# A fused attention, Fourier mixing and expert kernel on one core: raw weights loaded ahead, a second fold, split stores, factors on VectorE

## The chip, the cores and the metric

The kernel runs on one core of a Trainium2 chip. The metric is the device time of one execution in microseconds (us), the median of several runs. Engines are named as in the profile: PE (TensorE matmul), PEld (its weight loads), DVE (VectorE), ACT (ScalarE), POOL (GpSimd), SP (SyncE, which here issues most DMA transfers).

## The reference, cut to what matters

Three stages follow one another; B, H, S, D are 4, 8, 576, 64, so 2304 tokens of 512 features.

```python
# 1 attention, causal window of 128 with a linear bias per head
scores = where(mask, scale * q @ k.T - slope[h] * |i - j|, -1e9)
x = softmax(scores) @ v                      # -> (B, S, 512)
# 2 mixing and a dense MLP (w_ch1 512x2048, w_ch2 2048x512)
u  = x + real(fft(fft(x, axis=1), axis=2))
un = (u - mean(u)) / sqrt(var(u) + 1e-06)
x  = u + relu(un @ w_ch1) @ w_ch2
# 3 one of 8 experts a token (w1 512x1024, w2 1024x512), sticky routing
e  = argmax(x @ w_gate) if s == 0 or sigmoid(x @ w_local) < 0.5 else previous e
out = softmax(x @ w_gate)[e] * (relu(x @ w1[e]) @ w2[e])
```

The dense weights arrive as float64. The kernel reads them as pairs of 32-bit words ("raw words") and makes a high and a low float32 part of each; every dense product is then three matmuls (lines 162, 163, 164: high by high, high by low, low by high).

## The kernel before

**Attention** works on one batch at a time; its q and k come on SP (line 263), v too (line 265). Its rows leave in `xs`, folded about the middle of the sequence: block kt of `xs` holds rows `xa` and the mirrored rows `xb`.

**Mixing** (`mixing`, line 426) computes the real part of the two transforms as cosine and sine products. `fold` (lines 431 to 448) makes on DVE the sum and the difference of `xa` and `xb`, then adds (even part, line 445) and subtracts (odd part, line 446) the upper half of the 512 features onto the lower, mirrored. `zprod` (line 454) is the first product, over the sequence, in blocks of 128 features, with a last column, feature 256, apart in `zn`. The second product, over the features (lines 475 to 479), runs for each of three row blocks kb:

```python
for cs, ps in ((1, pz), (0, pc)):
    for db in range(2):
        nc.tensor.matmul(ps[0:n, 0:K2], lhsT=Z[cs][:, db, c0:c0 + n], rhs=tab2[:, cs, db], ...)
nc.tensor.matmul(pc[0:n, 0:K2], lhsT=zn[:, c0:c0 + n], rhs=alt, start=False, stop=True)
```

K2 is 257. A matmul in float32 shows as two records in the trace. Lines 482 to 489 combine the parts onto `xs` (DVE), and lines 491 to 502 store the rows as `ud`, 128 tokens a tile; one store holds rows 1 to 127 of tile 3 (line 493).

**Normalise** (line 546) loads `u` from `ud` on SP (line 553; not in the first group, whose rows are still in `xs`), takes statistics on DVE (lines 558, 560), makes the factor 1/sqrt(var) and the shift in 12 POOL operations (lines 565 to 573), applies them on ACT (line 577), transposes on PE (line 511) and splits into `xT` (ACT line 158, DVE line 159).

**The MLP** runs on nine groups of 256 tokens. `mlp_first` (line 595) does the first half of the 2048 hidden features with four weight chunks A of 256 and stores a partial sum `pd` (line 612); a later pass does the second half with four chunks B. `convert` (line 224) makes a quarter of a chunk from 512 KB of raw words: a load on SP (line 228) into one of RB = 2 buffers of the tag r64, a scaling on ACT (line 232), three operations on DVE (233 to 235), a cast on ACT (158) and a subtraction on POOL (159). A load waits for its buffer. Chunks live in the pools wpA and wpB, which hold four chunks each.

**Routing and experts.** Routing (lines 784 and following) follows each group of the second half. `early` (line 997) prepares the first 256 tokens of one expert while the last groups run: it loads that expert's weights (`expert_weights`, line 940), its list of slots (`slot_load`, line 981), turns it into row numbers (`slot_ids`, lines 990, 991), gathers the rows on POOL and transposes them on PE. Each `yield` gives way to the other work of the last groups; EL = 7 and EY = 8 count such steps.

**What sets the order.** The opening, mixing of batch 0 and normalise of group 0 (`opening`, line 676), is issued in the written order on PE, DVE, ACT and POOL. Afterwards attention, mixing, conversions and `mlp_first` are lanes of a table of due times, and a scheduler at build time fixes the order on each engine. Every engine then works strictly in that order; SP's queue too.

Of the kernel before, what the change touches and what calls it, by code (L numbers as in the profile page):

```python
# [10 lines left out]
F32 = mybir.dt.float32  # L11
# [12 lines left out]
DM = H * D  # L24
# [28 lines left out]
TB_ = 3  # L53
WB = 3
FL = 2
EY = 8
EL = 7
HB = 4
VL = 3
# [42 lines left out]
def constants():  # L102
    c = {}
    s = np.arange(3 * P).reshape(3, P).T
    k1 = np.arange(K1)
    ok = (s[:, :, None] <= HALF) & (k1[None, None, :] <= HALF)
    ang = (s[:, :, None] * k1[None, None, :]) % S
    tab1 = np.stack([np.where(ok, np.cos(2 * np.pi * ang / S), 0.0),
                     np.where(ok & ((2 * ang) % S != 0), np.sin(2 * np.pi * ang / S), 0.0)], 1)
    d = np.arange(2 * P).reshape(2, P).T  # L110
    k2 = np.arange(K2)
    ok = np.broadcast_to(k2[None, None, :] <= DM // 2, (P, 2, K2))
    ang = (d[:, :, None] * k2[None, None, :]) % DM
    tab2 = np.stack([np.where(ok, np.cos(2 * np.pi * ang / DM), 0.0),
                     np.where(ok & ((2 * ang) % DM != 0), np.sin(2 * np.pi * ang / DM), 0.0)], 1)
    c["tab1"] = tab1.astype(np.float32)
    c["tab2"] = tab2.astype(np.float32)
    c["alt"] = np.where(k2 <= DM // 2, 1.0 - 2.0 * (k2 % 2), 0.0).astype(np.float32)[None]
# [25 lines left out]
    empty = np.zeros((2, NSLOT, 4), np.float32)  # L144
    empty[0, :, 1] = NONE
    c["empty"] = empty
    c["zero"] = np.zeros((4 * P, DM), np.float32)
    return c


def build(ctx, tc, a, out):
# [55 lines left out]
    def weight_tiles(wp):  # L207
        return (wp.tile([P, 2, 4, CB], F32R, tag="w1", name="t1"), wp.tile([P, 2, CB // P, DM], F32R, tag="w2", name="t2"))

    def load_weights64(tiles, w1, w2, c, words):  # L210
        t1, t2 = tiles
        q = CB // 2
        for j in range(2):
            f0 = c * CB + j * q
            s = w1[:, 2 * f0:2 * (f0 + q)].rearrange("(k p) f -> p k f", p=P)
            convert(t1[:, 0, :, j * q:(j + 1) * q], t1[:, 1, :, j * q:(j + 1) * q], s, words)
            yield
        for j in range(CB // P):
            f0 = c * CB + j * P
            s = w2[f0:f0 + P].rearrange("p (k f) -> p k f", k=4)  # L220
            convert(t2[:, 0, j].rearrange("p (k f) -> p k f", k=4), t2[:, 1, j].rearrange("p (k f) -> p k f", k=4), s, words)
            yield

    def convert(hi, lo, src, words):

        k, n = hi.shape[1], hi.shape[2]
        r = wraw.tile([P, k, 2 * n], U32, tag="r64", name="r64", bufs=RB)
        nc.sync.dma_start(out=r, in_=src)
        w = r.rearrange("p k (n t) -> p k n t", t=2)
        wl, y = w[:, :, :, 0], w[:, :, :, 1]  # L230
        t = words().rearrange("p (k n) -> p k n", k=k)
# [13 lines left out]
    ps_s = c1.enter_context(pool("ps_s", 1, space=PSUM))  # L245

    tab1 = cst.tile([P, 2, 3, K1], F32, name="tab1")
    tab2 = cst.tile([P, 2, 2, K2], F32, name="tab2")
    alt = cst.tile([1, K2], F32, name="alt")

    def slab(shape, dt, name, tag, bufs):
        return sl.tile(shape, dt, tag=tag, name=name, bufs=bufs)

    HN = DM // 2
    NB = 5
    SC = -1.0 / math.sqrt(D)

# [168 lines left out]
    def mixing(b):  # L426
# [4 lines left out]
        def fold(kt):  # L431
# [22 lines left out]
        def zprod(part, kt):  # L454
            xf, n = zin[kt]
            for cs, db in part:
                w = P if db < 2 else 1
                if kt == 0:
                    pss[cs, db] = ps_g.tile([P, DM], F32, tag="g", name="zps")
                nc.tensor.matmul(pss[cs, db][0:w, 0:K1], lhsT=xf[0:n, cs, db * P:db * P + w], rhs=tab1[0:n, cs, kt], start=kt == 0, stop=kt == 2)  # L460
# [10 lines left out]
        for kb in range(3):  # L471
# [18 lines left out]
            row = lambda t: ud[GIDX[b, t]]  # L490
            if kb == 0:
                nc.sync.dma_start(out=row(0), in_=xs[0][:, 0])
                nc.sync.dma_start(out=row(3)[1:P], in_=xs[0][1:P, 1])
            elif kb == 1:
                nc.sync.dma_start(out=row(1), in_=xs[1][:, 0])
                nc.sync.dma_start(out=row(2), in_=xs[1][:, 1])
            else:
# [4 lines left out]
                nc.sync.dma_start(out=um[r + 32:r + 64], in_=xs[2][0:32, 1])  # L502
            if kb == 2:
                mixed[0] = b
            yield
# [40 lines left out]
    def normalise(gs, xT, us, src=None):  # L546
# [18 lines left out]
        nc.gpsimd.tensor_scalar_add(v0, mv[:, 0:n, 1], 1.0e-6)
        nc.gpsimd.tensor_tensor(out=v1, in0=v0, in1=half[:, 0:n], op=ALU.pow)
        for _ in range(2):
            nc.gpsimd.tensor_tensor(out=v2, in0=v1, in1=v1, op=ALU.mult)
            nc.gpsimd.tensor_tensor(out=v2, in0=v2, in1=v0, op=ALU.mult)
            nc.gpsimd.tensor_scalar(out=v2, in0=v2, scalar1=-0.5, scalar2=1.5, op0=ALU.mult, op1=ALU.add)  # L570
            nc.gpsimd.tensor_tensor(out=v1, in0=v2, in1=v1, op=ALU.mult)
        nc.gpsimd.tensor_tensor(out=v2, in0=mv[:, 0:n, 0], in1=v1, op=ALU.mult)
        nc.gpsimd.tensor_scalar_mul(v2, v2, -1.0)
        yield
        for i, g in enumerate(gs):
            un = us[i]
# [37 lines left out]
                for _ in pre:  # L614
                    yield ("piece", 0)

    chunksA = [weight_tiles(wpA) for c in range(FA // CB)]
    def tables():

        with tc.issue_after(last["load"].ins):  # L620
# [14 lines left out]

    def conversions():
        for c in range(FA // CB):
            yield from load_weights64(chunksA[c], a["w_ch1"], a["w_ch2"], c, lambda: sm.tile([P, 2 * CB], U32, tag="t64", name="t64", bufs=2))

    END = object()  # L640

# [96 lines left out]
    chunksB = [weight_tiles(wpB) for c in range(FA // CB, FF // CB)]  # L738

    room = lact.tile([P, 4, 2 * CB], U32, tag="xTe", name="t64", bufs=1)  # L740
    turns = iter(range(4 * FF // CB))
    for c in range(FA // CB, FF // CB):
        for _ in load_weights64(chunksB[c - FA // CB], a["w_ch1"], a["w_ch2"], c, lambda: room[:, next(turns) % 4]):
            pass

    wt8 = late.tile([P, E], F32, name="wt8")
# [456 lines left out]
```

## Time and profile before

| | |
|---|---|
| median of 3 runs | 1034.43 us (1032.81 to 1038.68) |
| profiled execution | 1039.1 us, span 1037.4 us, mean granted clock 0.959 |
| opening (0 to 84 us) | PE busy 67.30 us |
| attention and mixing of batches 1 to 3 beside the first MLP half (150 to 330) | PE busy 163.43 of 180 us |
| end of the first half, chunks B made (330 to 450) | PE busy 103.90 of 120 us |
| second half (450 to 700) | PE busy 246.79 of 250 us |
| its end, early expert (700 to 750) | PE busy 43.19 of 50 us |
| experts (750 to 1037) | PE busy 261.94 of 287 us |

The profile follows one execution; times of its instructions are from its own start. [...] Idle time of an engine stands in brackets with what ended it.

### The profile page before, as it was taken

Reading aid. Unit: us, or ns where it says so; the run is one execution under the profiler, and the core shown is the slowest. Engines: PE = TensorE matmul, PEld = TensorE weight load, DVE = VectorE, ACT = ScalarE, POOL = GpSimd, SP = SyncE. Lnnn points to the kernel's source line nnn. Section 1 sums busy time; section 2 is a strip of 40 time slices with the busy share of each in tenths; the row PEclk is TensorE's granted clock in tenths of the full one; section 3 lists DMA queues with packets and bytes.
Section 4 is the critical chain, followed back from the end, with each engine's and each line's share of the span. In section 5 each row is a group of like instructions: output and inputs, shape, how many; then the busy total and the mean of one; then the engine's idle time right before and its main releaser. Section 6 shows DMA issues by size and latency. Waiting matters only on the chain. (4 is left out here: it accounts for less than half of the span.)

```text
span 1037.4 us, 16275 instructions
## 1 busy us (share of the span) xinstructions
PE 946.8 (91%) x5959; PEld 770.6 (74%) x5959; DVE 520.1 (50%) x1286; ACT 381.3 (37%) x990; POOL 241.1 (23%) x358
## 2 busy tenths in 40 slices
PE   8877989889799888899999999997987999999993
PEld 4636666567568567688988888886876988888993
DVE  5777856636444455611133535354767644555510
ACT  5345654353252233421111111112436644454510
POOL 2245531230222034401011222222122212111100
PEclk9987999899989998999999999999999999999997
DMA  8345841342212155514344444444349745555300
GB/s 301 98 128 158 283 153 43 131 140 69 78 36 63 57 188 166 184 61 102 62 102 102 103 102 102 103 102 122 123 144 302 237 142 183 179 163 183 119 18 18
DMA packets 112103, 133.58 MB, mean 129 GB/s; under 512 B 16253, under 2 KB 79998, under 8 KB 111950
## 3 DMA queue, kind: packets, MB, share of 16 engines
q1 hardware_dynamic: 89166, 112.73, 34.0%
q0 software_dynamic: 22848, 19.72, 8.8%
q8 instruction: 49, 0.80, 0.3%
q14 instruction: 40, 0.33, 0.1%
HBM read 104.08 MB, written 31.23 MB: 130 GB/s over the span
## 5 line engine op out<-in xcount | busy, mean ns | idle before, releaser
L527 ACT ACTIVATE h<-hps 128x256 fp32r<-128x256 f32 x152 | 58.1, 382 | 263.7 <-PE hps L164 257.9
L528 DVE SCALAR_TENSOR_TENSOR h<-hps,h 128x256 fp32r<-128x256 f32 x152 | 63.7, 419 | 173.8 <-ACT h L527 173.5
L162 PE MATMUL acc<-t,h 128*128 128x512 f32 x304 | 127.8, 423 | 7.9 <-ACT h L527 7.0
L163 PE MATMUL acc<-t,h 128*128 128x512 f32 x304 | 123.6, 407 | 0.9 <-POOL t L159 0.8
L164 PE MATMUL acc<-t,h 128*128 128x512 f32 x304 | 120.5, 400 | 0.5 <-DVE h L528 0.5
L159 DVE TENSOR_TENSOR t<-we,t 128x512 fp32r<-128x512 f32 x144 | 93.8, 686 | 53.0 <-ACT t L158 52.3
L158 ACT CAST t<-we 128x512 fp32r<-128x512 f32 x144 | 82.6, 618 | 49.7 <-PE acc L164 24.9
L162 PE MATMUL hps<-xT,t 128*128 128x256 f32 x288 | 87.9, 305 | 4.9 <-DVE h L528 2.8
L162 PE MATMUL hps<-xTe,t 128*128 128x256 f32 (+5 forms) x288 | 87.0, 303 | 2.3 <-ACT xTe L158 2.3
L163 PE MATMUL hps<-xTe,t 128*128 128x256 f32 (+5 forms) x288 | 86.7, 301 | 0.3 <-DVE xTe L159 0.3
L164 PE MATMUL hps<-xTe,t 128*128 128x256 f32 (+5 forms) x288 | 86.9, 302 | 0.0
L164 PE MATMUL hps<-xT,t 128*128 128x256 f32 x288 | 84.4, 293 | 0.2 <-POOL t L159 0.2
L163 PE MATMUL hps<-xT,t 128*128 128x256 f32 x288 | 84.1, 292 | 0.0
L162 PE MATMUL hps<-xTb,t 128*128 128x256 f32 x288 | 83.2, 289 | 0.0
L164 PE MATMUL hps<-xTb,t 128*128 128x256 f32 x288 | 82.6, 287 | 0.0
L163 PE MATMUL hps<-xTb,t 128*128 128x256 f32 x288 | 82.2, 286 | 0.0
L345 ACT ACTIVATE t<-t,mx 128x128 f32<-128x128 f32 (+1 forms) x160 | 62.6, 394 | 47.3 <-DVE mx L338 43.1
L162 PEld LDWEIGHTS acc<-t,h 128*128 128x128 f32 x304 | 58.1, 193 | 25.5 <-ACT h L527 11.9
L162 PEld LDWEIGHTS hps<-xT,t 128*128 128x128 f32 x288 | 57.6, 200 | 16.1 <-DVE h L528 7.6
L162 PE MATMUL acc<-t,hE 128*128 128x512 f32 x168 | 67.6, 402 | 0.1
L164 PEld LDWEIGHTS acc<-t,h 128*128 128x128 f32 x304 | 57.7, 191 | 12.6 <-DVE h L528 1.1
L163 PEld LDWEIGHTS acc<-t,h 128*128 128x128 f32 x304 | 58.8, 194 | 10.3 <-POOL t L159 2.3
(260 smaller groups left out, 2039.8 us busy)
## 6 DMA issues: line engine op xcount, KB each, us to landing
we<-in_w SPq DMA_DIRECT2D x72, 512.0 KB
r<-in_w_ch SPq DMA_DIRECT2D x32, 512.0 KB
qkt<-in_qk SPq DMA_DIRECT2D x15, 642.0 KB
nd<-xT SPq DMA_DIRECT2D x18, 512.0 KB
xTb<-nd POOLq DMA_DIRECT2D x18, 512.0 KB, 6.0
vt<-in_v SPq DMA_DIRECT2D x16, 384.0 KB
pd<-y SPq DMA_DIRECT2D x18, 256.0 KB
ub<-ud SPq DMA_DIRECT2D x18, 256.0 KB
```

What stands on the lines that cost most here:

```text
L158: nc.scalar.copy(hi, src)
L159: (eng or nc.vector).tensor_tensor(out=lo, in0=src, in1=hi.bitcast(F32), op=ALU.subtract)
L162: nc.tensor.matmul(o, lhsT=wh, rhs=xh, start=start, stop=False, **kw)
L163: nc.tensor.matmul(o, lhsT=wh, rhs=xl, start=False, stop=False, **kw)
L164: return nc.tensor.matmul(o, lhsT=wl, rhs=xh, start=False, stop=stop, **kw)
L345: nc.scalar.activation(t[0:m, j], t[0:m, j], AF.Exp, bias=mx[0:m, j:j + 1], scale=-1.0, accum_out=sums[0:m, j:j + 1])
L527: nc.scalar.activation(h[:, 0, 0:n], hps[:, 0:n], AF.Relu)
L528: nc.vector.scalar_tensor_tensor(out=h[:, 1, 0:n], in0=hps[:, 0:n], scalar=0.0, in1=h[:, 0, 0:n].bitcast(F32), op0=ALU.max, op1=ALU.subtract)
```

## The change

1. Raw words of chunks A 0 to 2 are loaded during attention of batch 0, into tiles of wpA, chunk c's words where chunk c + 1 will be made. The raw words of chunks B 4 to 6 are loaded in the same way into wpB, issued after the last store of `ud`. The last chunk of each half keeps the two r64 buffers.
2. The factors of the first group are made on DVE: a starting value by an integer shift and subtraction, and three rounds of Newton, 17 operations, in place of 12 on POOL. Other groups stay on POOL.
3. The store of 127 rows becomes one of 112 and one of 15.
4. The features are folded a second time: four more DVE operations of 127 or 128 elements a fold. Even and odd frequencies are then made by separate products of 129 and 128 columns, written to every second column.
5. `early` loads the slots seven steps later, makes row numbers two steps after, and transposes after 5 steps in place of 8.

```diff
-    def load_weights64(tiles, w1, w2, c, words):
-        t1, t2 = tiles
+    def load_raw(c, wp=None):
+        if wp is not None:
+            raws[c] = [x[:, i] for x in (wp.tile([P, 2, 4, CB], U32, tag=g, name="rw") for g in ("w1", "w2")) for i in range(2)]
+        for i, s in enumerate(blocks64(c)):
+            if wp is None:
+                raws.setdefault(c, []).append(wraw.tile([P, 4, CB], U32, tag="r64", name="r64", bufs=RB))
+            nc.sync.dma_start(out=raws[c][i], in_=s)
+            yield
+
+    def load_weights64(chunks, i, c, wp, words):
+        t1, t2 = chunks[i] = weight_tiles(wp)
+        late_load = load_raw(c) if c not in raws else iter(())
...
             nc.vector.tensor_tensor(out=xo[0:n, 1:HN], in0=xo[0:n, 1:HN], in1=xo[0:n, DM - 1:HN:-1], op=ALU.subtract)
+            for y, add, sub, o in ((xe, ALU.add, ALU.subtract, 0), (xo, ALU.subtract, ALU.add, 1)):
+                nc.vector.tensor_tensor(out=y[0:n, ZC[1]:ZC[1] + P], in0=y[0:n, o:P + o], in1=y[0:n, HN - o:HN - P - o:-1], op=sub)
+                nc.vector.tensor_tensor(out=y[0:n, o:P], in0=y[0:n, o:P], in1=y[0:n, HN - o:HN - P:-1], op=add)
...
-                for db in range(2):
-                    nc.tensor.matmul(ps[0:n, 0:K2], lhsT=Z[cs][:, db, c0:c0 + n], rhs=tab2[:, cs, db], start=db == 0, stop=db == 1 and cs == 1)
-            nc.tensor.matmul(pc[0:n, 0:K2], lhsT=zn[:, c0:c0 + n], rhs=alt, start=False, stop=True)
+                for odd in range(2):
+                    o = ps[0:n, odd:K2:2]
+                    nc.tensor.matmul(o, lhsT=Z[cs][:, odd, c0:c0 + n], rhs=tab2[:, 2 * cs + odd, 0:P + 1 - odd], start=True, stop=cs == 1 or odd == 1)
+                    if cs == 0 and odd == 0:
+                        nc.tensor.matmul(o, lhsT=zn[:, c0:c0 + n], rhs=alt, start=False, stop=True)
...
-                nc.sync.dma_start(out=row(3)[1:P], in_=xs[0][1:P, 1])
+                nc.sync.dma_start(out=row(3)[1:P - 15], in_=xs[0][1:P - 15, 1])
+                nc.sync.dma_start(out=row(3)[P - 15:P], in_=xs[0][P - 15:P, 1])
...
+        eng = nc.gpsimd if src is us else nc.vector
...
+            r = v1.bitcast(I32)
+            eng.tensor_single_scalar(r, v0.bitcast(I32), 1, op=ALU.logical_shift_right)
+            eng.tensor_scalar(out=r, in0=r, scalar1=-1.0, scalar2=float(0x5F3759DF), op0=ALU.mult, op1=ALU.add)
+        for _ in range(2 if src is us else 3):
...
         for n, _ in enumerate(attention(0)):
+            if n == 9:
+                for _ in load_raw(0, wpA):
+                    pass
+            if n == 14:
+                for c in range(1, nA - 1):
+                    for _ in load_raw(c, wpA):
+                        pass
...
+    with tc.issue_after(last["ud"].ins):
+        for c in range(nA, nA + nB - 1):
+            for _ in load_raw(c, wpB):
+                pass
...
         pre_.add(expert_weights(-1, e))
         yield
+        for _ in range(EL):
+            yield
         x = slot_load(e * CAP, TM, 1)
-        for _ in range(EL):
+        for _ in range(2):
             yield
```

The order on ACT in the opening, about the normalisation of the first group. Names: `r` and `rw` are raw words being scaled, `u<-x,v` is the normalisation, `tps` the transposes. Before:

```order
L577 ACTIVATE u<-x,v 128x512
L345 ACTIVATE t,sums<-t,mx 65x128 x2
L158 CAST xT<-tps 128x4x128
L577 ACTIVATE u<-x,v 128x512
L232 ACTIVATE r_896<-r_896 128x512
L158 CAST xT<-tps 128x4x128
L232 ACTIVATE r_886<-r_886 128x512
```

and now:

```order
L620 ACTIVATE u<-x,v 128x512
L163 CAST xT<-tps 128x4x128
L620 ACTIVATE u<-x,v 128x512
L163 CAST xT<-tps 128x4x128
L258 ACTIVATE rw<-rw 128x512
L385 COPY w<-pt 128x512 x2
```

The scaling of raw words that stood between the two casts to xT, and an exponential of attention, no longer stand between the normalisations.

The order on SP after the last store of the last batch's mixing (`u` loads of normalise, `nd` and `pd` stores, raw words `r` and `rw`). Before:

```order
L502 DMA ud_78<-x 32x512
L228 DMA r_4702<-in_w_ch 128x1024
L228 DMA r_4710<-in_w_ch 128x1024
L553 DMA u<-ud_73 128x512
L579 DMA nd_107<-xT 1024x1x128
L553 DMA u<-ud_78 128x512
L579 DMA nd_108<-xT 1024x1x128
L228 DMA r_4718<-in_w_ch 128x4x256
L228 DMA r_4726<-in_w_ch 128x4x256
L612 DMA pd_86<-y 128x512
L612 DMA pd_88<-y 128x512
L553 DMA u<-ud_74 128x512
```

and now:

```order
L622 DMA nd_108<-xT 1024x1x128
L588 DMA u<-ud_78 128x512
L235 DMA rw<-in_w_ch 128x1024 x2
L235 DMA rw<-in_w_ch 128x4x256
L655 DMA pd_86<-y 128x512
L655 DMA pd_88<-y 128x512
L235 DMA rw<-in_w_ch 128x4x256
L235 DMA rw<-in_w_ch 128x1024 x2
L235 DMA rw<-in_w_ch 128x4x256 x2
L235 DMA rw<-in_w_ch 128x1024 x2
L588 DMA u<-ud_74 128x512
```

Seven loads of raw words now stand between the partial sums of a group and the next `u` load, where none stood.

The order on SP where the early expert begins (`we` are its weights, `ids` its slots, `p_` the partial sums of a group). Before:

```order
L940 DMA we<-in_w 128x4x256
L940 ISA
L940 DMA we<-in_w 128x2x512
L1029 DMA p__6882<-pd_94 128x512
L1062 DMA x2d<-x_7156 128x512
L1029 DMA p__6887<-pd_95 128x512
L981 ISA
L981 DMA ids<-slots_115 128x2x4
L940 ISA
L940 DMA we<-in_w 128x4x256
```

and now:

```order
L1118 DMA x2d<-x_7199 128x512
L994 ISA
L994 DMA we<-in_w 128x4x256
L1085 DMA p__6932<-pd_95 128x512
L994 ISA
L994 DMA we<-in_w 128x2x512
L1118 DMA x2d<-x_7202 128x512
L994 ISA
L994 DMA we<-in_w 128x4x256
L1035 ISA
L1035 DMA ids<-slots_115 128x2x4
```

The slot load stood ahead of the expert's third weight load (the last row shown) and now stands behind its fifth.

## Rows read from the trace of the kernel before

**Rows 1.** The page, part 1: busy time, share of the span and instructions.

```profile
PE 946.8 (91%) x5959; PEld 770.6 (74%) x5959; DVE 520.1 (50%) x1286; ACT 381.3 (37%) x990; POOL 241.1 (23%) x358
```

**Rows 2.** Windows: from:to, length, busy us of each engine, granted clock, DMA share, GB/s.

```profile
core 0: us, PE busy (x) PEld busy (x) DVE busy (x) ACT busy (x) POOL busy (x), PEclk, DMA share, GB/s
190.00:200.00 10.00, 5.98 (x52) 4.41 (x48) 4.31 (x10) 2.90 (x12) 2.79 (x5) 0.77 0.37 124
274.00:276.00 2.00, 2.00 (x18) 2.00 (x18) 0.00 (x0) 0.00 (x0) 0.00 (x0) 1.00 0.07 26
276.00:290.00 14.00, 5.84 (x29) 2.25 (x27) 4.82 (x12) 4.29 (x15) 4.58 (x15) 0.67 0.20 72
290.00:300.00 10.00, 10.00 (x58) 6.62 (x58) 5.27 (x13) 3.67 (x12) 1.47 (x3) 0.78 0.21 67
420.00:430.00 10.00, 9.89 (x59) 7.61 (x58) 8.09 (x15) 5.77 (x12) 3.64 (x3) 1.00 1.00 312
720.00:730.00 10.00, 4.29 (x15) 3.78 (x16) 4.80 (x23) 3.03 (x7) 3.38 (x4) 0.72 0.62 193
```

**Rows 3.** Timeline of DVE, 186 to 292: start, us, instruction, [idle before, releaser].

```profile
194.92 0.42 DVE L401 TENSOR_TENSOR x<-xps,rec 128x256 f32<-128x256 f32 x1 [3.79 <-DMA ud<-x]
...
280.18 0.69 DVE L558 BATCH_NORM_STATS2 st<-u 128x6 f32<-128x512 f32 x1 [10.76 <-DMA u<-ud]
```

**Rows 4.** Timeline of PE at the end of the opening.

```profile
78.85 1.11 PE L511 MATMUL tps<-ident,u 128*128 128x128 f32 x4 [1.39 <-ACT u L577]
...
83.25 0.58 PE L162 MATMUL hps<-xT,t 128*128 128x256 f32 x1 [2.00 <-ACT xT L158]
```

**Rows 5.** Timeline of POOL in the opening: the first and the last of the factors' 12 operations.

```profile
68.78 0.23 POOL L565 TENSOR_SCALAR v<-mv 128x2 f32<-128x2 f32 x1 [5.62 <-DVE mv L560]
...
75.20 0.24 POOL L573 TENSOR_SCALAR v<-v 128x2 f32<-128x2 f32 x1
```

**Rows 6.** Timeline of DVE in the routing: two dependent tiny operations.

```profile
754.70 0.17 DVE L808 TENSOR_TENSOR oh<-oh,wt 128x16 f32<-128x16 f32 x1
754.90 0.17 DVE L813 TENSOR_REDUCE rmx<-oh 128x2 f32<-128x16 f32 x1
```

**Rows 7.** Timeline of ACT in the opening, the second cast to xT.

```profile
82.07 0.65 ACT L232 ACTIVATE r<-r 128x512 f32<-128x512 f32 x1 [3.27 <-DMA r<-in_w_ch]
82.62 0.57 ACT L158 CAST xT<-tps 128x512 fp32r<-128x512 f32 x1
```

**Rows 8.** Timeline of DVE in the first fold of batch 0.

```profile
46.97 0.68 DVE L441 TENSOR_TENSOR xf<-x 128x512 f32<-128x512 f32 x1
47.58 0.41 DVE L445 TENSOR_TENSOR xf<-xf 128x255 f32<-128x255 f32 x1
47.91 0.41 DVE L446 TENSOR_TENSOR xf<-xf 128x255 f32<-128x255 f32 x1
```

**Rows 9.** Timeline of PE in the first group, where it waits for converted weights.

```profile
137.69 0.73 PE L162 MATMUL acc<-t,h 128*128 128x512 f32 x2 [0.65 <-ACT t L158]
...
139.17 0.50 PE L163 MATMUL acc<-t,h 128*128 128x512 f32 x1 [0.63 <-POOL t L159]
```

**Rows 10.** Timeline of PE, batch 2: a block's second product, what follows it, attention's transposes.

```profile
270.17 1.03 PE L478 MATMUL pz<-tab,z 128*128 128x257 f32 x4
...
272.63 0.28 PE L326 MATMUL s<-first,id 128*128 128x128 bf16 x2
...
275.65 0.60 PE L354 MATMUL pt<-ident,t 128*128 128x128 f32 x4
```

**Rows 11.** Forms of line 478: duration ns min/median/max, first and last start.

```profile
L478 PEld LDWEIGHTS pz<-tab,z x48: 108/188/193, 58.6 to 360.4; 128*128 128x128 f32 x32, 128*33 128x33 f32 x16
```

**Rows 12.** Waits from 360 to 450 us: total us, times, longest.

```profile
PE tps L511 <- ACT u L577: 5.1, 2, 3.4
PE acc L162 <- ACT h L527: 4.3, 2, 2.9
```

**Rows 13.** SP's waits from 655 to 800 us; PE's timeline near 720.

```profile
SPq L981 <- DMA slots<-ent,su: 10.2, 4, 6.1
...
725.72 0.38 PE L795 MATMUL pn<-ident,lt 10*128 10x10 f32 x2 [6.43 <-ACT lt L791]
```

More of the change, by code (lines that the diff above doesn't have):

```diff
@@ L55 @@
 FL = 2
-EY = 8
+EY = 5
 EL = 7
@@ L109, in constants @@
                      np.where(ok & ((2 * ang) % S != 0), np.sin(2 * np.pi * ang / S), 0.0)], 1)
[L110 to L115, printed above, removed]
+    d = np.arange(P)[:, None]
+    k2 = np.arange(P + 1)[None, :]
+    tab2 = np.zeros((P, 4, P + 1))
+    for odd in range(2):
+        ok = 2 * k2 + odd <= DM // 2
+        ang = (d * (2 * k2 + odd)) % DM
+        tab2[:, odd] = np.where(ok, np.cos(2 * np.pi * ang / DM), 0.0)
+        ang = ((d + odd) * (2 * k2 + odd)) % DM
+        tab2[:, 2 + odd] = np.where(ok & ((2 * ang) % DM != 0), np.sin(2 * np.pi * ang / DM), 0.0)
+    tab2[P - 1, 3] *= 0.5
     c["tab1"] = tab1.astype(np.float32)
     c["tab2"] = tab2.astype(np.float32)
-    c["alt"] = np.where(k2 <= DM // 2, 1.0 - 2.0 * (k2 % 2), 0.0).astype(np.float32)[None]
+    c["alt"] = (1.0 - 2.0 * (np.arange(P + 1) % 2)).astype(np.float32)[None]
     q = np.arange(P)[:, None]
@@ L208, in weight_tiles, with blocks64 @@
         return (wp.tile([P, 2, 4, CB], F32R, tag="w1", name="t1"), wp.tile([P, 2, CB // P, DM], F32R, tag="w2", name="t2"))
-    def load_weights64(tiles, w1, w2, c, words):
-        t1, t2 = tiles
+    raws = {}
+    def blocks64(c):
+        w1, w2 = a["w_ch1"], a["w_ch2"]
         q = CB // 2
@@ L214, in load_weights64, with convert @@
             f0 = c * CB + j * q
-            s = w1[:, 2 * f0:2 * (f0 + q)].rearrange("(k p) f -> p k f", p=P)
-            convert(t1[:, 0, :, j * q:(j + 1) * q], t1[:, 1, :, j * q:(j + 1) * q], s, words)
-            yield
+            yield w1[:, 2 * f0:2 * (f0 + q)].rearrange("(k p) f -> p k f", p=P)
         for j in range(CB // P):
             f0 = c * CB + j * P
-            s = w2[f0:f0 + P].rearrange("p (k f) -> p k f", k=4)
-            convert(t2[:, 0, j].rearrange("p (k f) -> p k f", k=4), t2[:, 1, j].rearrange("p (k f) -> p k f", k=4), s, words)
-            yield
[L224 to L228, printed above, removed]
+            yield w2[f0:f0 + P].rearrange("p (k f) -> p k f", k=4)
+    def load_raw(c, wp=None):
[5 more added lines that the diff above has]
+            nc.sync.dma_start(out=raws[c][i], in_=s)
+            yield
+    def load_weights64(chunks, i, c, wp, words):
+        t1, t2 = chunks[i] = weight_tiles(wp)
+        q = CB // 2
+        late_load = load_raw(c) if c not in raws else iter(())
+        for _ in range(RB - 1):
+            next(late_load, None)
+        for i in range(4):
+            next(late_load, None)
+            r = raws[c][i]
+            if i < 2:
+                convert(t1[:, 0, :, i * q:(i + 1) * q], t1[:, 1, :, i * q:(i + 1) * q], r, words)
+            else:
+                convert(t2[:, 0, i - 2].rearrange("p (k f) -> p k f", k=4), t2[:, 1, i - 2].rearrange("p (k f) -> p k f", k=4), r, words)
+            yield
+    def convert(hi, lo, r, words):
         w = r.rearrange("p k (n t) -> p k n t", t=2)
         wl, y = w[:, :, :, 0], w[:, :, :, 1]
-        t = words().rearrange("p (k n) -> p k n", k=k)
+        t = words().rearrange("p (k n) -> p k n", k=4)
         nc.scalar.activation(y.bitcast(F32), y.bitcast(F32), AF.Copy, scale=BIAS)
@@ L254, in build @@
     HN = DM // 2
+    ZC = (0, HN + D, P)
     NB = 5
@@ L459, in zprod @@
                     pss[cs, db] = ps_g.tile([P, DM], F32, tag="g", name="zps")
-                nc.tensor.matmul(pss[cs, db][0:w, 0:K1], lhsT=xf[0:n, cs, db * P:db * P + w], rhs=tab1[0:n, cs, kt], start=kt == 0, stop=kt == 2)
+                nc.tensor.matmul(pss[cs, db][0:w, 0:K1], lhsT=xf[0:n, cs, ZC[db]:ZC[db] + w], rhs=tab1[0:n, cs, kt], start=kt == 0, stop=kt == 2)
                 if kt == 2:
@@ L476, in mixing @@
             for cs, ps in ((1, pz), (0, pc)):
[L477 to L479 removed]
+                for odd in range(2):
+                    o = ps[0:n, odd:K2:2]
+                    nc.tensor.matmul(o, lhsT=Z[cs][:, odd, c0:c0 + n], rhs=tab2[:, 2 * cs + odd, 0:P + 1 - odd], start=True, stop=cs == 1 or odd == 1)
+                    if cs == 0 and odd == 0:
+                        nc.tensor.matmul(o, lhsT=zn[:, c0:c0 + n], rhs=alt, start=False, stop=True)
             cb_ = slab([P, 3, K2], F32, "cmb", "m", MB)
@@ L501, in mixing @@
                 nc.sync.dma_start(out=um[r:r + 32], in_=xs[2][0:32, 0])
-                nc.sync.dma_start(out=um[r + 32:r + 64], in_=xs[2][0:32, 1])
+                last["ud"] = nc.sync.dma_start(out=um[r + 32:r + 64], in_=xs[2][0:32, 1])
             if kb == 2:
@@ L564, in normalise @@
         v0, v1, v2 = (v[:, i, 0:n] for i in range(3))
[L565 to L573, printed above, removed]
+        eng = nc.gpsimd if src is us else nc.vector
+        eng.tensor_scalar_add(v0, mv[:, 0:n, 1], 1.0e-6)
+        if src is us:
+            eng.tensor_tensor(out=v1, in0=v0, in1=half[:, 0:n], op=ALU.pow)
+        else:
+            r = v1.bitcast(I32)
+            eng.tensor_single_scalar(r, v0.bitcast(I32), 1, op=ALU.logical_shift_right)
+            eng.tensor_scalar(out=r, in0=r, scalar1=-1.0, scalar2=float(0x5F3759DF), op0=ALU.mult, op1=ALU.add)
+        for _ in range(2 if src is us else 3):
+            eng.tensor_tensor(out=v2, in0=v1, in1=v1, op=ALU.mult)
+            eng.tensor_tensor(out=v2, in0=v2, in1=v0, op=ALU.mult)
+            eng.tensor_scalar(out=v2, in0=v2, scalar1=-0.5, scalar2=1.5, op0=ALU.mult, op1=ALU.add)
+            eng.tensor_tensor(out=v1, in0=v2, in1=v1, op=ALU.mult)
+        eng.tensor_tensor(out=v2, in0=mv[:, 0:n, 0], in1=v1, op=ALU.mult)
+        eng.tensor_scalar_mul(v2, v2, -1.0)
         yield
@@ L615, in mlp_first @@
                     yield ("piece", 0)
-    chunksA = [weight_tiles(wpA) for c in range(FA // CB)]
+    chunksA = [None] * nA
     def tables():
@@ L637, in conversions @@
         for c in range(FA // CB):
-            yield from load_weights64(chunksA[c], a["w_ch1"], a["w_ch2"], c, lambda: sm.tile([P, 2 * CB], U32, tag="t64", name="t64", bufs=2))
+            yield from load_weights64(chunksA, c, c, wpA, lambda: sm.tile([P, 2 * CB], U32, tag="t64", name="t64", bufs=2))
     END = object()
@@ L737, in build @@
     lact = c2.enter_context(pool("lact", 2, reuse_waits="tile"))
-    chunksB = [weight_tiles(wpB) for c in range(FA // CB, FF // CB)]
+    chunksB = [None] * nB
     room = lact.tile([P, 4, 2 * CB], U32, tag="xTe", name="t64", bufs=1)
     turns = iter(range(4 * FF // CB))
+    with tc.issue_after(last["ud"].ins):
+        for c in range(nA, nA + nB - 1):
+            for _ in load_raw(c, wpB):
+                pass
     for c in range(FA // CB, FF // CB):
-        for _ in load_weights64(chunksB[c - FA // CB], a["w_ch1"], a["w_ch2"], c, lambda: room[:, next(turns) % 4]):
+        for _ in load_weights64(chunksB, c - nA, c, wpB, lambda: room[:, next(turns) % 4]):
             pass
```

4 lines of the change are left out of this document (2 added, 2 removed).

## The prediction

> **What bounds the kernel now.** I read the page first: PE is busy 946.8 us, 91% of the span [rows 1], so only what shortens PE's work or fills its idle stretches can move the end. I then took windows of ten us and marked those in which PE was idle or its granted clock under 1 [rows 2]. [...] The opening ends for PE with the first hidden matmul of the first group at 83.25 us [rows 4].
>
> The profiled execution took 1039.1 us (span 1037.4), 4.7 over the median of 1034.43. I work out differences in it and take them off the median. Two executions of one kernel differ by up to 0.6% in the runs shown, so 0.5%, 5 us, is about what can be told from no change.
>
> **Opening.** The normalisation's factors run on POOL from 68.78 to 75.44, 6.66 us [rows 5]. On DVE they are 17 operations, each on the result of the one before; two dependent tiny ones there start 0.20 us apart [rows 6], so 17 × 0.20 = 3.4 and 3.3 us go. The second block's cast to xT could start when its transposes end, 78.85 + 1.11 = 79.96 [rows 4], and started at 82.62, behind an ACT scaling that waited for raw words [rows 7]. The scaling now stands behind the casts and its words come in attention(0): 2.6 us more. Against that the second fold puts 12 operations into the folds that the first product waits for. A 512-element operation takes 0.61 us from start to start and a 255-element one 0.33 [rows 8], on a line 0.19 for 128 elements; I take 0.20, so 2.4 us. The sum is −3.5; what is next late is the attention scores that share PE there, and I take **−3**. Bounds: −6 where the folds hide, +2.5 where each tiny operation costs double and the cast gains nothing. The eight extra raw loads stand on SP ahead of the query loads of batch 1, which are wanted only after the opening: nothing, and at worst part of that +2.5.
>
> **Raw words of chunks 1 and 2.** In 84 to 150 us the conversions come late for PE twice, by 0.65 and 0.63 us [rows 9]. Their words lie ready now: **−1** (0 to −1.3). The conversion's arithmetic on ACT, DVE and POOL stays as it is.
>
> **The store in two parts.** The store of 127 rows (254 KB) of batch 2 is the only traffic in 274 to 276: DMA share 0.07, one engine of 16, 26 GB/s [rows 2], so about 254 / 26 = 10 us. Behind it the u load landed after DVE had waited 10.76 us; DVE works in order, so the combine of the mixing and with it PE stood. In batch 1 DVE waited 3.79 us before it overwrote an x that the store was still reading [rows 3]. If 112 rows go over many engines, this wait goes. Batch 1: 4.0 us idle, and 5.98 busy at a mean clock of 0.77, 5.98 × 0.23 = 1.4, together 5.4; I take **−5** (0 to −5.4). Batch 2: idle 14 − 5.84 = 8.2; the clock's part is 5.84 × 0.33 = 1.9 and 10 × 0.22 = 2.2: 12.3. A u load still has to land, some 2 us, so **−10** (0 to −12.3). Batch 3 has no such row and gets nothing. The trace has no store of 112 or 15 rows. [...]
>
> **The second product.** For each of nine blocks in batches 1 to 3 (batch 0 lies in the opening) PE runs ten matmul records, from 270.17 to 272.63, 2.46 us [rows 10]. With half the columns the nearest row is a transpose of 128 columns with its own weight load, 0.60 / 4 = 0.15 each [rows 10]: 1.5 us, 1.0 saved, 9 us in all. The lower bound of a record is half of the old one's step, 0.105 (1.4 saved); the upper its weight load, 0.19 [rows 11] (0.56 saved). The 36 added fold operations are 7.2 us of DVE, half idle over the span, but the first product waits for the last of each batch; I let 4 of 7.2 show. **−5**, from −12.7 (9 × 1.41) to +2.2 (7.2 − 9 × 0.56). [...]
>
> **Raw words of the second half.** Between 360 and 450 us PE waited 5.1 us for the normalisation's ACT step and 4.3 for a hidden ACT step [rows 12]; conversions of four chunks stand on those engines at that time. Three chunks (12 loads of 512 KB) are now issued as soon as the last `ud` store is. I take **−3** (−9 if both waits go; +12 in the rival below).
>
> **The early expert.** The slot load waits on SP for its list's writes, 10.2 us in four waits, the longest 6.1 [rows 13]; the weight loads behind it on SP, ACT's casts of them and the route's copy behind the casts make PE wait 6.43 [rows 13]. The load now stands behind seven more yields, and so behind more weight loads, when the list is long written. Beside the 6.4 idle, 4.29 × 0.28 = 1.2 us went to the clock [rows 2]. DVE's cast now waits for a load issued two yields earlier, at most a us or so; the expert's transposes come one hidden block sooner and their gathers stand as before. **−6** (0 to −7.6).
>
> **Sum.** −3 − 1 − 5 − 10 − 5 − 3 − 6 = −33: 1039.1 − 33 = 1006 for such an execution, and 1034.4 − 33 = **1001 us** for the median.
>
> **Rivals.**
> - *More goes than I count* (987 us, 0.13): opening −6, first raw words −1.3, store −17.7, product −9, later raw words −6, early −7.6, together −47.6; for it, half-clock stretches follow each idle one; against, what is next late is not in the trace.
> - *The product is paced by its weight loads* (0.12): 9 × 0.56 − 4 = 1 gained in place of 5, so 1005 us. For it the 0.19 [rows 11], against it the 0.15 of the transposes.
> - *The raw words' burst collides* (0.14): from 365 us twelve loads go out. At the 312 GB/s of 420 to 430, where the DMA engines were full [rows 2], the seven tiles of 512 KB ahead of one u load take 11.8 us. Then +12 stands for −3: 1034 − 30 + 12 = 1016 us.
> - *The store doesn't spread* (0.08): the change doesn't do what it says if 112 or 15 rows still take one engine. 112 of them would take 224 KB / 26 GB/s = 8.6 us, and batch 1 and 2 keep nearly all: 1034 − 33 + 14 = 1015 us.
> - *Slower* (0.03): the burst holds up u loads of three groups in turn, each in front of DVE's statistics, behind which DVE's part of the hidden step stands, so PE idles and restarts at half clock. In batch 2, 8.2 idle us cost 12.3, so 1.5 per idle us: three waits of 11.8 cost 53, and 1034 − 30 + 53 = 1057 us. It decides from 30 / 1.5 = 20 us of such waits. Against it: the loads spread behind stores that wait for PE, and a wait for all of the burst happens once.
>
> **Numbers.** Forecast 0.48, those rivals 0.13, 0.12, 0.14, 0.08 and 0.03, and 0.02 that all parts are hidden anyway. 984 to 1020 us takes in the forecast with its bounds, the paced product, burst and store cases and most of the first rival; about 0.12 is left out. Faster by over 0.5%: 0.95; within: 0.02; slower: 0.03.
>
> **What would show it.** The first hidden matmul near 80 us and no ACT wait for raw words before it; no DVE wait over 3 us on `u<-ud` or a store near 190 and 270, and PE's idle of 4 and 8 us gone; the ten product records of one block in about 1.5 us; PE waiting under 1 us for the route near 720; in 360 to 450 waits of PE no larger than before. A wait of DVE on `u` of 10 us there, or a store at 0.07 of the DMA engines, would make the forecast wrong by 12 to 15 us; PE idle in new places with the old ones closed would say that the time only moved.

## The result, and the profile after

The changed kernel took 1023.49 us (median of 4, 1022.20 to 1026.62) beside 1036.56 us for the kernel before: a ratio of 0.9866 with a 95% interval of 0.9828 to 0.9904. Run again on another chip it gave 0.9841 (0.9797 to 0.9885). By these two ratios it is faster by 14 and 16 us. The forecast was 33 us less, 1001 us, with a range of 984 to 1020.

The table divides the profiled executions at the same instructions, from start to start in the timelines; "fold b" is the first fold operation of batch b, and a group ends with the first of its two `pd` stores. Each column is one execution; "again" is the changed kernel on the other chip, and where the two differ one sees what an execution's own scatter is. b_store and s_early are introduced below: the kernel before with only its store split, and the change with only the split store and the early expert's order.

| us | before | after | after, again | b_store | s_early |
|---|---|---|---|---|---|
| fold 0 to first statistics | 20.6 | 28.2 | 29.4 | 20.6 | 20.6 |
| to first normalisation on ACT | 8.5 | 9.3 | 9.3 | 8.5 | 8.5 |
| to first hidden matmul | 7.8 | 5.4 | 5.4 | 5.4 | 5.4 |
| to end of group 0 | 61.8 | 53.7 | 55.8 | 59.9 | 60.7 |
| fold 0 to fold 1 | 114.0 | 117.8 | 121.1 | 109.7 | 110.5 |
| fold 1 to fold 2 | 75.9 | 71.1 | 70.5 | 70.6 | 69.6 |
| fold 2 to fold 3 | 96.4 | 81.3 | 81.6 | 84.3 | 84.0 |
| fold 3 to end of the first half's last group | 166.0 | 170.1 | 166.5 | 166.0 | 166.6 |
| from there to first expert output | 280.4 | 274.3 | 273.6 | 279.0 | 273.9 |

So the gain lies between fold 1 and fold 3 (about 20 us) and at the early expert (6 to 7). The opening lost 4 to 7. The end of the first half lost 4.1 in one execution and 0.5 in the other; what that stage is without its early loads follows below.

**What went as forecast.** DVE's waits for u loads between 84 and 320 us, the answer to [rows 3], all lie under 2.1 us; where 10.76 stood, near 280, it is now this one:

```profile
272.38 0.69 DVE L593 BATCH_NORM_STATS2 st<-u 128x6 f32<-128x512 f32 x1 [1.49 <-DMA u<-ud]
```

The windows of the same places, which answer to [rows 2], show PE nearly full in batches 1 and 2 (the first two lines), at a granted clock of 1.00, which is the profile's share of TensorE's full speed; at the early expert (the last two) 2.7 of 20 us are idle:

```profile
186.00:206.00 20.00, 19.35 (x170) 13.87 (x167) 16.59 (x38) 11.49 (x46) 6.43 (x12) 1.00 0.46 140
272.00:282.00 10.00, 10.00 (x82) 7.51 (x81) 8.03 (x19) 4.25 (x19) 5.04 (x16) 1.00 0.28 97
704.00:714.00 10.00, 7.31 (x38) 5.44 (x38) 8.44 (x12) 5.34 (x12) 3.47 (x3) 0.83 0.74 204
714.00:724.00 10.00, 10.00 (x66) 8.81 (x66) 8.49 (x34) 3.55 (x8) 2.41 (x2) 1.00 0.63 190
```

A block's product on PE, [rows 10], runs from 271.63 to 273.13, the 1.50 us of the forecast:

```profile
271.63 0.61 PE L510 MATMUL pz<-tab,z 128*128 128x129 f32 x4
272.07 0.39 PE L510 MATMUL pc<-tab,z 128*128 128x129 f32 x2
272.39 0.48 PE L512 MATMUL pc<-alt,zn 1*128 1x129 f32 x2
272.80 0.49 PE L510 MATMUL pc<-tab,z 128*128 128x128 f32 x2
273.13 0.28 PE L353 MATMUL s<-first,id 128*128 128x128 bf16 x2
```

The sum is right by luck in part. The forecast's 0.15 us a record is the 0.60 us of four transposes divided by four, and the 0.60 holds the full 0.27 us of the last one; their starts lie (0.60 − 0.27) / 3 = 0.11 apart. By the lines above the first four records start 0.11 us apart ((272.07 − 271.63) / 4); the two of the one-row product (line 512) take 0.41 together, where the forecast counted 0.30.

**What went the other way: the opening.** DVE's timeline of the first folds, [rows 8], shows operations of batch 1's attention (lines 361, 363, 365) among them, five in all. From the first fold at 49.05 to the operation after the last at 61.59 it takes 12.5 us, where it took 6.8 before (46.31 to 53.07):

```profile
49.05 0.74 DVE L465 SCALAR_TENSOR_TENSOR xf<-x,inner 128x512 f32<-128x512 f32 x1
...
50.98 0.29 DVE L476 TENSOR_TENSOR xf<-xf 128x128 f32<-128x128 f32 x1
51.18 0.69 DVE L365 TENSOR_REDUCE mx<-t 128x4 f32<-128x512 f32 x1
51.77 0.29 DVE L477 TENSOR_TENSOR xf<-xf 128x128 f32<-128x128 f32 x1
...
55.58 0.68 DVE L363 SCALAR_TENSOR_TENSOR t<-s,bias 128x512 f32<-128x512 f32 x1
...
61.05 0.43 DVE L361 COPY_PREDICATED s<-mask,s 65x260 f32<-65x260 int32 x1 [0.45 <-PE s L357]
61.39 0.28 DVE L477 TENSOR_TENSOR xf<-xf 33x127 f32<-33x127 f32 x1
61.59 0.41 DVE L259 TENSOR_SCALAR t<-rw 128x512 uint32<-128x512 uint32 x1
```

Then the factors, [rows 5]: on DVE they run from 78.79 to 82.14, 3.35 us as worked out. But a conversion stands behind them on DVE, and ACT, in order, casts that conversion before it normalises:

```profile
78.79 0.17 DVE L602 TENSOR_SCALAR v<-mv 128x2 f32<-128x2 f32 x1
...
81.97 0.17 DVE L616 TENSOR_SCALAR v<-v 128x2 f32<-128x2 f32 x1
...
85.30 0.69 DVE L261 SCALAR_TENSOR_TENSOR t<-rw,t 128x512 uint32<-128x512 uint32 x1
```

ACT's and PE's timelines: ACT waits 10.63 us for that conversion, PE 12.11 for ACT, and the first hidden matmul comes at 91.96 in place of 83.25 [rows 4]. Of these 8.7 us 2.7 lie ahead of the first fold (49.05 in place of 46.31) and 6.0 behind it:

```profile
86.03 0.62 ACT L163 CAST t<-t 128x512 fp32r<-128x512 f32 x1 [10.63 <-DVE t L261]
86.55 0.81 ACT L620 ACTIVATE u<-x,v 128x512 f32<-128x512 f32 x1
```

```profile
87.41 1.11 PE L546 MATMUL tps<-ident,u 128*128 128x128 f32 x4 [12.11 <-ACT u L620]
...
91.96 0.56 PE L167 MATMUL hps<-xT,t 128*128 128x256 f32 x1
```

**And the end of the first half.** PE's waits from 360 to 450 us, the answer to [rows 12], grew from 12.7 (the 9.4 of those rows, 2.8 for `hps` and 0.5) to 17.1 us, and to 15.7 in the other execution of the changed kernel; the window of one group (368 to 409) shows POOL busy 20 of 41 us:

```profile
PE acc L167 <- ACT h L562: 7.4, 3, 4.2
PE hps L167 <- DVE h L563: 5.9, 5, 2.6
PE tps L546 <- ACT u L620: 3.8, 1, 3.8
```

```profile
368.00:409.00 41.00, 29.26 (x152) 25.30 (x151) 26.43 (x40) 18.65 (x36) 20.09 (x32) 0.83 0.45 150
```

### The profile page after: what moved, and what is told of

It reads as the page before. It is cut to its first block, busy times and chain, and to the rows that moved or that the text cites. A ratio compares the mean times of both kernels' runs of the same rounds, so it can differ in the third digit from the quotient of the medians.

```text
span 1022.3 us, 16308 instructions
## 1 busy us (share of the span) xinstructions
PE 930.9 (91%) x5958; PEld 765.5 (75%) x5959; DVE 534.9 (52%) x1351; ACT 381.6 (37%) x990; POOL 239.5 (23%) x346
## 5 line engine op out<-in xcount | busy, mean ns | idle before, releaser
L164 DVE TENSOR_TENSOR t<-we,t 128x512 fp32r<-128x512 f32 x144 | 96.4, 703 | 55.3 <-ACT t L163 52.6
L169 PE MATMUL hps<-xTb,t 128*128 128x256 f32 x288 | 82.3, 286 | 0.0
L168 PEld LDWEIGHTS acc<-t,h 128*128 128x128 f32 x304 | 58.3, 192 | 12.1 <-POOL t L164 5.0
```

Of the source, the lines that this page charges most:

```text
L164: (eng or nc.vector).tensor_tensor(out=lo, in0=src, in1=hi.bitcast(F32), op=ALU.subtract)
L168: nc.tensor.matmul(o, lhsT=wh, rhs=xl, start=False, stop=False, **kw)
L169: return nc.tensor.matmul(o, lhsT=wl, rhs=xh, start=False, stop=stop, **kw)
```

## The experiments

**Undoing one part of the changed kernel.** The ratios stand beside 0.9866 and 0.9841 of the changed kernel; intervals are about 0.004 to 0.006 to each side, so a difference under 0.005 isn't shown by the ratio alone. The quoted text ahead of each result is what was expected; "theory", "case" and "rival" below are its words. Stages come from one profiled execution each.

*Early raw words of chunks 0 to 2 taken out.*

```diff
-            if n == 9: ... load_raw(0, wpA)
-            if n == 14: ... load_raw(c, wpA) for chunks 1 and 2
```

> The changed kernel with the raw words of chunks 0 to 2 loaded as before (two r64 buffers, during the conversions); all else as changed. Theory 1, the early loads cost the opening: they stand on SP ahead of batch 1's queries, so batch 1's scores fall behind into the folds; then the first hidden matmul comes near 86 us in place of 92, attention rows leave the folds, and the time is 1017 to 1024 us, the conversions of the first group being slower again by up to 8. Theory 2, the cost is the longer chain on DVE (folds, then factors, then a conversion ACT waits for): the first hidden matmul stays near 92 and the time rises to 1025 to 1032.

Ratio 0.9840 (0.9784 to 0.9896), no shown difference. Fold 0 to statistics stayed at 27.7, so theory 1 falls for the opening; the longer time of theory 2 did not come either. Group 0 took 59.8 us in place of 53.7, and fold 0 to fold 1 117.4 in place of 117.8. What the words give group 0 doesn't reach fold 1. Fold 1 to fold 2 took 77.1 in place of 71.1; the granted clock there was 0.50 from 180 to 190 us, which comes back below.

*Early raw words of the second half taken out.*

```diff
-    with tc.issue_after(last["ud"].ins): ... load_raw(c, wpB)
```

> The changed kernel with the raw words of chunks 4 to 6 loaded as before. Theory 1, the burst costs the transition: from the end of group 3 to the end of group 7 it takes 105 us in place of 110, and the time is 1016 to 1020 us. Theory 2, what was lost there comes from conversions and factors that queue on ACT, DVE and POOL in any order of loads: within 2 us of 1023.5.

Ratio 0.9785 (0.9732 to 0.9838), 1015.4 us, just under the times of theory 1. Fold 3 to the end of the last group took 161.9 in place of 170.1 and 166.5, and PE's waits from 360 to 450 us are 12.9: theory 1.

*Factors back on POOL.*

```diff
-        eng = nc.gpsimd if src is us else nc.vector
+        eng = nc.gpsimd
```

> The changed kernel with the first group's factors on POOL as before. Theory 2 (the factors on DVE push the third block's combine and a conversion back, for which ACT waits before it normalises): DVE reaches that conversion 3.4 us sooner, the factors end 3.3 us later, so the normalisation starts 1 to 2 us sooner or at the same time: 1022 to 1024 us. Rival, the factors on DVE are worth their 3.3 us: 1026 to 1028.

Ratio 0.9848 (0.9794 to 0.9902): the rival, 3 us slower, didn't come. Statistics to normalisation fell from 9.3 to 6.9 us. ACT still waits for the conversion first, 7.24 us in place of 10.63, casts it, and then waits 0.86 more for the factors:

```profile
82.60 0.81 ACT L620 ACTIVATE u<-x,v 128x512 f32<-128x512 f32 x1 [0.86 <-POOL v L616]
```

*The conversion moved behind the normalisation.*

```diff
-        next(conv)
         for _ in nrm:
             pass
         next(conv)
+        next(conv)
```

> The changed kernel with the third quarter of chunk 0's conversion issued after the normalisation in the opening instead of before it. Theory 2: ACT no longer waits 10.6 us for DVE's conversion before normalising, so normalisation starts near 82.3 in place of 86.6 and the first hidden matmul near 88; the time is 1019 to 1021 us, if the third quarter is not then late for the first group (rival: it is, and the time stays within 1 us of 1023.5).

Ratio 0.9813 (0.9761 to 0.9865), lower, but by under 0.005 beside 0.9841. Statistics to normalisation fell to 4.9 us (this execution began its folds 2.6 us later, so the start itself lies at 85.90 and not near 82.3), and the releaser is the last factor. The factors' price on DVE is thus the conversion that stands behind them there and that ACT casts first:

```profile
85.90 0.81 ACT L620 ACTIVATE u<-x,v 128x512 f32<-128x512 f32 x1 [7.34 <-DVE v L616]
```

*Second fold taken out* (tables and products of 257 columns as before).

```diff
-            for y, add, sub, o in (...): nc.vector.tensor_tensor(...) twice
```

> The changed kernel without the second fold: one fold of the features and products of 257 columns as before, all else as changed. Theory 2: in the opening the folds take 6.8 us in place of 12.5 and no attention operation stands between them, so the normalisation starts 4 to 6 us sooner; in batches 1 to 3 a block's product takes 2.46 in place of 1.50 us, 8.6 us in all, and 7.2 us of DVE work go. The two nearly cancel: 1022 to 1028 us. Rival, the forecast's term (5 us net gain and little in the opening): 1029 to 1032.

Ratio 0.9865 (0.9824 to 0.9906): they cancel. Fold 0 to statistics is back at 20.6, statistics to normalisation is then 11.0, with the same conversion as the last wait, and fold 2 to fold 3 takes 83.7 in place of 81.3.

*The 127-row store in one piece.*

```diff
-                nc.sync.dma_start(out=row(3)[1:P - 15], in_=xs[0][1:P - 15, 1])
-                nc.sync.dma_start(out=row(3)[P - 15:P], in_=xs[0][P - 15:P, 1])
+                nc.sync.dma_start(out=row(3)[1:P], in_=xs[0][1:P, 1])
```

> The changed kernel with the 127-row store in one piece as before. If the split was worth what the stages show (5 us in batch 1, about 13 in batch 2): DVE waits over 8 us for a u load near 270 to 280 again and the time is 1036 to 1042. Rival, the earlier finish of batch 2 comes from the shorter products and the changed order: 1024 to 1030.

Ratio 1.0049 (1.0022 to 1.0076): without the split the rest of the change is slower than the kernel before, by 0.5%. DVE's old waits are back:

```profile
207.09 0.42 DVE L428 TENSOR_TENSOR x<-xps,rec 128x256 f32<-128x256 f32 x1 [4.75 <-DMA ud<-x]
...
292.52 0.69 DVE L592 BATCH_NORM_STATS2 st<-u 128x6 f32<-128x512 f32 x1 [10.75 <-DMA u<-ud]
```

*The early expert's old order.*

```diff
-EY = 5
+EY = 8
-        for _ in range(EL):
-            yield
         x = slot_load(e * CAP, TM, 1)
-        for _ in range(2):
+        for _ in range(EL):
```

> The changed kernel with the early expert's slot load and transposes in the old places. If the term held: PE waits about 6 us for the route's copy near 710 again and the time is 1028 to 1031. Rival, the weights are late there anyhow: 1023 to 1025.

The ratio, 0.9869 (0.9834 to 0.9904), doesn't show it. The stage does: 281.1 us from the first half's last store to the first expert output, in place of 274.3, with PE's wait back:

```profile
718.31 0.38 PE L849 MATMUL pn<-ident,lt 10*128 10x10 f32 x2 [4.85 <-ACT lt L845]
```

**Repairs.** *No early words for the second half, and the conversion late* (both edits above).

> The changed kernel without the early loads for the second half, and with the third quarter of chunk 0 converted after the first normalisation. If the two costs are separate they add: 8 and 5 us off 1023.5, 1009 to 1012. Rival, both are paid by the same stretch of conversions: 1014 to 1016.

Ratio 0.9800 (0.9762 to 0.9838), no better than the first edit alone: they don't add, as the rival had it. *The changed kernel again:*

> The changed kernel itself once more, beside the next three on one chip, as their measure: 0.983 to 0.990 of the kernel before.

0.9841, as expected. *Batch 1's attention kept out of the folds:*

```diff
+        ends.append(last["fold"].ins)
```

> The changed kernel, but nothing of batch 1's attention may be issued ahead of the last fold operation of batch 0. If the attention operations that stand between the folds make the rest of the fold's price in the opening (7.6 us, of which the 12 operations themselves are 2.4), first fold to first statistics takes 23 to 25 us in place of 28.2 and the time is 3 to 5 us less than the changed kernel's. Rival, the wait for the first product is set by PE's clock and the longer DVE chain only: 27 to 28 us there and the same time.

Fold 0 to statistics fell to 24.0 us, as the first case had it, and the ratio, 0.9878 (0.9826 to 0.9930), shows no gain. Of the 5.4 us won beside the 29.4 of the same chip, 2.6 went at once: statistics to normalisation rose to 11.9, for ACT now had batch 1's exponentials and the conversion to do first. Fold 1 to fold 2 then took 76.4 us in place of 70.5. There the granted clock was 0.50, though PE was busy all through, as the window shows beside that of the changed kernel on the same chip (second line):

```profile
180.00:190.00 10.00, 10.00 (x26) 3.66 (x24) 0.72 (x2) 3.38 (x13) 0.85 (x2) 0.50 0.00 0
180.00:190.00 10.00, 10.00 (x58) 5.46 (x56) 4.76 (x10) 6.00 (x20) 1.56 (x4) 1.00 0.03 12
```

The run without the early words of chunks 0 to 2 shows the same 0.50 and the same longer stage. With one profiled execution of each it stays open whether the clock falls there every time; so neither ratio tells by itself what its edit is worth in the opening. *All three:*

> All three repairs at once: no early loads for the second half, the third quarter of chunk 0 converted after the normalisation, the folds of batch 0 ahead of batch 1's attention. By the stages of the earlier runs 8 + 4.4 + 4 less than the changed kernel, about 1007 where that takes 1023.5; rival, the opening's gains are paid back by the conversions and only the 8 are left: 1015.

Ratio 0.9792 (0.9748 to 0.9837), 1015.4 us: the rival.

**One part added to a simple base.** *The kernel before with only its store split* (the edit of the store above, the other way).

> The kernel before with only its 127-row store made in two parts of 112 and 15 rows. If the split carries most of the change: the stages of batch 1 and 2 shorten by 15 to 19 us and the time is 0.982 to 0.986 of the kernel before. Rival, without the shorter products and the other edits the gain is half: 0.990 to 0.993.

Ratio 0.9793 (0.9748 to 0.9837), 1015.1 us: more than the most expected, and 3 us less than the whole change on the same chip (1018.4), a difference that the ratios alone don't show. No wait of DVE for a store is left, and its waits for u are at most 1.74 us; where 10.76 stood it is now this one:

```profile
261.77 0.69 DVE L559 BATCH_NORM_STATS2 st<-u 128x6 f32<-128x512 f32 x1 [1.72 <-DMA u<-ud]
```

The gain shows in the stages of three batches, 0, 1 and 2: 4.3, 5.3 and 12.1 us. In the opening a load of raw words, issued at 73.75 (before at 73.46), lets ACT scale at 78.99, not at 82.07 [rows 7]:

```profile
78.99 0.67 ACT L232 ACTIVATE r<-r 128x512 f32<-128x512 f32 x1
```

*Split and early expert's order together* (s_early; s_early2 is the same again; both are the changed kernel's text with its other parts taken out).

> Of the change only the split store and the early expert's order. If the two add: 0.979 of the kernel before less 6 us, 0.972 to 0.976, about 1009 where the kernel before takes 1036.5, and no single added part makes it faster. Rival, the early expert's 6 us are lost in what follows: 0.978 to 0.980.

> The base once more, on the same chip: 0.968 to 0.977 of the kernel before.

Ratios 0.9727 (0.9679 to 0.9774) and 0.9786 (0.9750 to 0.9823), 1011.9 and 1013.3 us; the second lies outside what was expected of it. The early part's stage fell from 279.0 to 273.9 and 273.6; beside the 0.9793 of the split alone the ratios don't show it. No version was shown to be faster than this one.

*Raw words of chunks 0 to 2, second fold, factors on DVE, raw words of the second half, each alone on that base:*

> Base plus the early raw words of chunks 0 to 2. If these words cost the opening by what they push back on SP (batch 1's queries): first fold to fold of batch 1 takes over 3 us more than in the base, and the time is 2 to 5 us more. Rival, they pay by themselves and only the other parts cost: the first group ends 6 us sooner and the time is 3 to 6 us less.

0.9743 (0.9698 to 0.9787). Group 0 took 55.5 us in place of 60.7, fold 0 to fold 1 111.2 in place of 110.5; neither case: gained, and not on the path to the end.

> Base plus the second fold. By the stages: 7 us lost in the opening, 3 us gained in batch 3, some in 1 and 2: the same time as the base or up to 4 us more. Rival, the forecast's net gain of 5 us.

0.9734 (0.9687 to 0.9781), the same as the base: 5.9 lost to the first statistics (6.3 to fold 1), 2.9 gained from fold 2 to fold 3, and 7.0 after it (159.7 in place of 166.6).

> Base plus the first group's factors on DVE. If the conversion that ACT waits for sets the normalisation: statistics to normalisation takes 9 to 11 us in place of 8.5 and the time is the same to 3 us more. Rival, the forecast's 3.3 us less.

0.9773 (0.9731 to 0.9816). Statistics to normalisation took 11.0 in place of 8.5, and fold 0 to fold 1 113.2 in place of 110.5. The forecast's 3.3 us less did not come.

> Base (split store, early expert's order) plus the early raw words of the second half. If they cost by themselves: batch 3's first fold to the last store of the first half takes 4 to 8 us more than in the base, POOL is busy over 18 us in one group, and the time is 0.005 to 0.008 of the kernel before above the base. Rival, they cost only behind the rest of the change: within 0.002 of the base.

0.9822 (0.9782 to 0.9862) beside 0.9786 of the base on the same chip: between the two cases. The stage took 168.4 in place of 165.9, less than expected and less than the 3.6 us by which the changed kernel's two executions differ there. In one group POOL is busy 20.49 of 38 us, where in the base's (34 us) it is 13.37:

```profile
367.00:405.00 38.00, 29.98 (x158) 25.53 (x158) 28.32 (x43) 17.57 (x34) 20.49 (x24) 0.85 0.36 119
```

```profile
366.00:400.00 34.00, 27.93 (x143) 23.50 (x144) 20.76 (x35) 15.24 (x30) 13.37 (x19) 0.85 0.52 161
```

Adding the four differences, each to the base on its own chip (0.0016, 0.0007, 0.0046, 0.0036), to the mean of the base's two ratios, 0.9757, gives 0.9862; the changed kernel has 0.9866 and 0.9841. Each of the four is within its intervals of nothing. That together they lose is shown by the whole: the mean of the changed kernel's ratios lies 0.0097 over the base's, some 10 us. Their order among themselves is shown only by the stages.

## Why the prediction was wrong

- **Opening (−3; came out +6.0 and +7.2 from the first fold to the first hidden matmul).** The prices of single operations held: 0.20 us for a small fold, 3.35 for the factors. The step that failed is "what is next late is the attention scores". Next late was ACT's order: it casts a conversion before it normalises, and DVE makes that conversion only after the factors and the third block's combine. Work taken from an idle POOL was put in front of it: alone on the base this turned 8.5 us into 11.0. The fold's 2.4 became 5.9 to 8.8, because the new order set attention operations between the folds (3.4 when they were kept out); the order rows of the opening were read on ACT alone, and those of DVE would have shown it.
- **Opening, the words for ACT (−2.6 within the −3; about 0).** The 2.6 us for ACT's wait for raw words did go (7.8 became 5.4), but the forecast gave them to the early words alone: b_store has the 5.4 with the loads in the old place, and the changed kernel with its store in one piece has it too. Either edit alone is enough, so beside the split store the early words gave nothing here. The folds also began at 46.7 to 51.7 us in the twelve executions with the early words of chunks 0 to 2, and at 46.2 to 47.2 in the eight without them; the forecast put these loads at nothing, and whether they cause it wasn't tried.
- **Raw words of chunks 1 and 2 (−1; about 0).** Larger than thought in its place (4 to 6 us of group 0), and fold 0 to fold 1 doesn't show it (111.2 beside 110.5 on the base). The step missed was to ask what the second group waits for.
- **Store (−15; −21).** Mechanism right, price too low: the term left out batch 0's store, which cost 4.3 us, and batch 2's gain took in the whole 12. Both terms (−5 and −10) rest on 112 rows going over many engines, which no run of the kernel before shows. In the changed kernel the two parts and the 256 KB store issued just ahead of them are the traffic from 268 to 270 us of batch 2: 257 GB/s at a mean DMA share of 0.74 (1.00 from 269.0 to 269.5), where the one store had 26 GB/s at 0.07 [rows 2]. DVE's wait for the u load behind it fell from 10.76 to 1.49 us; the 2 us or so left for that load was the author's estimate. How many engines each part takes isn't shown.
- **Second product (−5; about 0).** 1.50 us a block as forecast, in part by luck. The rival's pace of one weight load, 0.19 us a record, didn't come: four records start 0.11 us apart. Half the columns took half the time, 0.11 in place of 0.22 (the four of 1.03 us in [rows 10] start 0.22 apart). The loss is the folds in the opening, which the forecast booked there at 2.4 us, under half of their price.
- **Raw words of the second half (−3; +4.6 and +8.2 in their stage, +2 on the base, which is within scatter).** The three versions without these loads and with the split store lie at 0.9785 to 0.9800, the eight runs of the changed kernel and its variants that keep both at 0.9813 to 0.9878. The rival "the burst collides" had the sign, not the mechanism: u loads aren't late (DVE's only wait for one between 320 and 500 us is 0.18). The step that failed is that words which lie ready would shorten PE's two waits: with `hps` the waits grew from 12.7 to 17.1 us, and without the loads they are 12.9. The words being there, the build-time order sets conversions closer together, and one group's hidden steps on ACT and DVE queue behind them and behind POOL. That this is the reason is read from the windows; a version with the same loads and the old spacing wasn't tried.
- **Early expert (−6; −5 to −7 in its stage).** As forecast; PE's wait of 6.43 for the route is gone, and comes back as 4.85 with the old order.

Of the 33 us, then, the store's 15 came as 21 and the early expert's 6 as 5 to 7; the 12 that the other parts were to add came out as a loss of some 10.

## What to carry to other kernels

Count a store's rows: one store of 127 rows a batch cost 21 us in three batches, and two transfers of 112 and 15 cured it. Before work is moved to another engine, even from one that is nearly idle, list what stands behind it there and which in-order engine waits for that; the price of the moved operations is the smaller part. A load made early pays only if what waits for it lies on the path to the end; and where a change gives a scheduler more freedom, read the new order on every engine, not only on the one that the change was meant for.

## What the runs showed of the hardware

- The 127-row store delayed transfers issued after it. The same load of 512 KB took from issue to ACT's scaling 82.07 − 73.46 = 8.6 us with that store issued 9 us ahead of it, and at most 78.99 − 73.75 = 5.2 in b_store, where ACT reached the scaling without a wait. The two kernels differ in the store alone.
- A DVE operation took 1.1 us longer beside POOL. In the changed kernel's DVE timeline the same operation of line 259 takes 0.42 us and, while POOL's three subtractions run (from 385.04, 4.58 us), 1.52; what holds it up there isn't shown:

```profile
386.96 1.52 DVE L259 TENSOR_SCALAR t<-rw 128x512 uint32<-128x512 uint32 x1
388.51 1.65 DVE L260 SCALAR_TENSOR_TENSOR t<-rw,t 128x512 uint32<-128x512 uint32 x1
...
390.80 0.42 DVE L259 TENSOR_SCALAR t<-rw 128x512 uint32<-128x512 uint32 x1
```

```profile
385.04 4.58 POOL L164 TENSOR_TENSOR t<-t,t 128x512 fp32r<-128x512 f32 x3 [0.70 <-ACT t L163]
```

- TensorE's granted clock was 0.50 in a stretch in which PE was busy: from 180 to 190 us in the run with batch 1's attention kept out of the folds, with PE busy 10.00 of 10 us, and 1.00 in the same stretch of the changed kernel on the same chip. In the changed kernel's first profiled execution it was 0.66 from 180 to 185 us, with PE busy 5.00 of 5, after 1.00 from 165 to 180 with PE busy 13.95 of 15; why the clock fell stays open.
